# Narrower matmuls for the rest blocks of a two-layer MoE, an earlier request for a count, and scatters spread further apart

## The chip, the cores and the metric

The kernel runs on one core of one Trainium2 chip. The metric is the device time of one execution in microseconds (us); less is better. A core has TensorE (PE in the profile; its weight loads stand apart as PEld), VectorE (DVE), ScalarE (ACT), GpSimd (POOL) and SyncE (SP, which here only issues DMAs). Each runs its own queue of instructions in order, and they meet at semaphores.

## What is computed

A linear attention with decay, then two layers of a mixture of experts with one expert for each token. Cut to what matters:

```python
ret = (scale * q @ k.T) * Dmat               # 8 batches, 8 heads, 576 positions, 64 wide
x = (ret @ v)                                # as 4608 tokens of 512 columns
# layer 1, and layer 2 with other weights and a bias by modality:
logits = x @ w_gate
e_idx = argmax(logits)                       # one of 8 experts for each token
for e in range(8):
    h = maximum(x[e_idx == e] @ w1[e], 0)    # 512 -> 1024
    out[e_idx == e] = gate * (h @ w2[e])     # 1024 -> 512
```

With the reference's inputs the experts of the first layer get 602, 613, 589, 549, 586, 487, 608 and 574 tokens. The kernel takes tokens in blocks of 256 (pairs) and, for what is left over, in one block of up to 128 (the rest block). So each expert here has two pairs; all but expert 5 also have a rest, of 90, 101, 77, 37, 74, 96 and 62 tokens (the second pair of expert 5 covers the last 231). In the second layer two experts share all tokens (2315 and 2293).

## The kernel before, in words

**Attention and routing** (`attention_and_routing`). 36 chunks of 128 tokens, in four pairs of batches of nine chunks each. One chunk passes several engines: POOL scales v (`v_scale`, tile `vs`) and cuts the scores to a triangle (`a_cut`, two instructions on tile `a`); PE computes scores (`pa`), states (`pS`), output (`po`) and the transposed output with the gate's logits (`px`, `turned`); ACT and DVE move results between PSUM and SBUF (`og`, `xr`, `Sb`, `lg`). The order is written out by hand: every piece of work has a due time in chunks (`PLAN`), the list is sorted by it, and every engine gets its instructions in that order. Routing goes by groups of two to five chunks (they start at chunks 0, 4, 9, 13, 18, 22, 27, 31 and 34). When the last chunk of a group has its logits, `route` runs fifteen small steps (on DVE: `mx`, `dl`, `wq`, `m`, `oh`, `zz` and so on); then each chunk's rows are written to their expert's place in DRAM by an indirect DMA that POOL issues (`scatter`, tile `xs`, L178). The due times of a group's scatters are its last step plus 0.225 chunk, and 0.428 chunk from one to the next (`SCATTER`).

**The change over.** At the end of attention `counts` writes the experts' counts as small integers into `reg1`: pairs in columns 0 to 7, the rest flag in 8 to 15. All engines meet at a barrier, read their registers, and PE runs eleven matmuls (`READY`) on constants until the first rows arrive.

**The experts** (`experts`). Five engine programs, each walking through 16 positions (`P_`; 0 to 7 are the experts of the first layer, 8 to 15 those of the second), with branches on the counts. `walk` calls `unit(P_, s, w, ...)`: slot 0 and slot 1 are pairs of 256 columns, slot 2 is the rest block, always 128 columns in the first layer; in the second it may also be 64. For one unit:
- PE: the first product, `quarter(g)` for g = 0 to 3, each 24 matmuls (eight of 128 rows of w1, high and low halves in three combinations) into `ph[g]`; then, for each block of 128 tokens, the second product of 24 matmuls of 512 columns into `py`. For the second product the tokens are the stationary side, so its time doesn't depend on the columns of the first. Before each six matmuls of the first block it waits for a piece of hT (`h_full`).
- ACT: Relu of `ph[g]` to `hT` (high half, L1093); then `back`: Square of `py` and the scaled copy to `x2row`.
- DVE: the low half of `hT` (L1205); routing of the tokens for the second layer (`choose`, which ends in `oh`, and `place`); conversions of the next expert's weights (`conv`, `wb`); then `back` for each block, in the same queue.
- SP: loads and transposes, among them `x2T`, the transposed rows of finished blocks, which PE needs for the second layer's logits (L969).

The routing of a finished block is woven into the next units: in a rest block PE computes the logits of the pair's first block after the first six second-product matmuls and its ranks (L974, L975, which need `oh`) at the block's end; in a second pair the logits come after the third and fourth quarter, and the first ranks after the first six second-product matmuls.

In position 6 (`asked`) the order of the second layer's experts is settled ahead of time: after the first pair PE computes the counts so far (`counts(cums)`, L980), for which it waits for `cnt_ask` from DVE; DVE's `order()` turns them into an order. In the unit of the first pair DVE runs four pieces of hT, two conversions (`brought`), then the semaphore `cnt_ask`, then two `back`s, then `order()`.

Pieces of a program that are seldom taken (`co.unlikely`) are put at the end of the engine's program: a conditional jump leads there and another one back.

Of the kernel before, what the change touches and what calls it, by code (L numbers as in the profile page):

```python
# [14 lines left out]
I32 = mybir.dt.int32  # L15
AF = mybir.ActivationFunctionType
ALU = mybir.AluOpType
# [5 lines left out]
P = 128  # L23
# [15 lines left out]
GATES = -5.2, -1.440, -2.415, 1.091  # L39
WARM = 15  # L40
STEPS, RANKS, STEP, HURRY = 15, 10, 0.1684, {27: 0.1, 31: 0.055, NT - 2: 0.04}
SCATTER = 0.225, 0.428
HALVES = (38.2, 38.3, 38.32, 38.34, 38.36, 38.38, 38.4, 38.42), 43.0
READY = 11

# [37 lines left out]
def attention_and_routing(tc, st, I, K):  # L83

    nc = tc.nc
# [10 lines left out]
    ones, tri = K["ones"], K["tri"]  # L96
# [287 lines left out]
    for gr in groups:  # L384
        last = max(gr.start + n + PLAN["lg"] for n, x in enumerate(gr.items))
        chain = route(gr)
        for k in range(STEPS):
            last += HURRY.get(gr.start, STEP)
            if k == RANKS and gr.start < NT - 2:
                last = int(last - 0.045) + 1.045  # L390
            add(last, next, chain, None)
        for n, x in enumerate(gr.items):
            add(last + SCATTER[0] + n * SCATTER[1], scatter, x)
    def counts():

        pm = ps.tile([P, 512], F32, tag="pS", name="pm_cnt")
        nc.tensor.matmul(pm[:, 0:8], ones, cum[0], start=True, stop=True)
        cf = one.tile([1, 8], F32, tag="cf", name="cf")
        c2 = one.tile([1, 1, 8], I32, tag="c2", name="c2")
        reg = K["reg1"]  # L400
        nc.vector.tensor_copy(reg[:, 16:24], pm[0:1, 0:8])
        nc.vector.tensor_tensor(cf, pm[0:1, 0:8], col("eR")[0:1], op=ALU.subtract)
        nc.vector.tensor_scalar(c2[:, 0], cf, 127.0, None, op0=ALU.add)
        nc.vector.tensor_scalar(reg[:, 0:8], c2[:, 0], 8, None, op0=ALU.logical_shift_right)
        nc.vector.tensor_scalar(reg[:, 8:16], c2[:, 0], 6, 2, op0=ALU.logical_shift_right, op1=ALU.bitwise_and)


    fetch, high, low = first_weights(nc, I, K, lambda n: three.tile([P, 512], F32, tag="dqvk"[n % 4] + "n", bufs=6, name=f"w0s{n}"))
# [75 lines left out]
def experts(nc, st, I, K, out):  # L484
# [38 lines left out]
    take = T.take  # L523
    NP = 2 * E
    EP = 2
    PAIR, FULL, SMALL = 2 * P, P, P // 2

    def cols(P_, w):

# [2 lines left out]
    def count1(eng, R_, x):  # L532

        if x < E:
            eng.reg_load(R_["np"][x], reg1[0:1, x:x + 1])
            eng.reg_load(R_["od"][x], reg1[0:1, 8 + x:9 + x])

    def count2(eng, R_, x):

# [107 lines left out]
    def walk(co, R_, P_, unit, none=None, conv=None, first=None):  # L647

        eng, pairs, od = co.eng, R_["np"][P_ % E], R_["od"][P_ % E]
        if P_ < E:  # L650
            block, after = co.label("block"), co.label("after")

            def without():
                if none:
                    none()
                if first and P_ == 0:
                    first()
                for q in range(2 if conv and P_ == 0 else 0):
                    conv(0, 2 + q)
                if conv:  # L660
                    for slot in range(2):
                        for q in range(2):
                            brought(eng, R_, P_, conv, slot, q)

            def other():
                with when(eng, pairs, "GT", 1):
                    unit(P_, 1, PAIR, True, 1)
                    pairs_from(eng, R_, P_, unit, 2)
                if conv:
                    with eng.Else():  # L670
                        for q in range(2):
                            brought(eng, R_, P_, conv, 1, q)
            co.unlikely(pairs, "LT", 1, without, block)
            unit(P_, 0, PAIR, False, 0)
            co.unlikely(pairs, "NE", 2, other, block)
            unit(P_, 1, PAIR, True, 1)
            co.to(block)
            co.jump(od, "EQ", 0, after)
            unit(P_, 2, FULL, False)
            co.to(after)  # L680
            return
        with when(eng, pairs, "GT", 0):
            unit(P_, 0, PAIR, False, 0)
            with when(eng, pairs, "GT", 1):
                unit(P_, 1, PAIR, True, 1)
                pairs_from(eng, R_, P_, unit, 2)
        if none:
            with eng.Else():
                none()
        with when(eng, od, "EQ", 2):  # L690
            unit(P_, 2, FULL, False)
        with eng.Else():
            with when(eng, od, "EQ", 1):
                unit(P_, 2, SMALL, False)
        if conv:
            rest(eng, R_, P_, conv)
# [39 lines left out]
    def asked(P_, slot):  # L736

        return P_ == E - 2 and slot == 0

    def registers(rs, eng, tag, names, full=None):  # L740

        reg = lambda x: rs.enter_context(eng.register(f"{tag}{x}"))
        R_ = {x: reg(x) for x in names}
        for n in ("np", "od", "left"):
            R_[n] = [reg(f"{n}{x}") for x in range(E)]
        if full:
            eng.reg_load(R_["np"][0], reg1[0:1, 0:1])
            with when(eng, R_["np"][0], "GT", 1):
                full()
            eng.reg_load(R_["od"][0], reg1[0:1, 8:9])  # L750
        else:
            count1(eng, R_, 0)
        return R_

    with nc.Block() as block:
# [204 lines left out]
        def _(pe):  # L960
            with ExitStack() as rs:
# [69 lines left out]
                            counts(cums)  # L1031

                for n in range(READY):
                    pe.matmul(py[1], K["ones"], K["ones"].unsqueeze(1).to_broadcast([P, 4, P]), start=True, stop=True)
                pe.reg_mov(was, 0)
                co = Course(pe, "pe")
                for P_ in range(NP):
# [92 lines left out]
        def _(ve):  # L1130
            ch = Chain(ve, T, "dve")
            tt, ts, stt, tr = ve.tensor_tensor, ve.tensor_scalar, ve.scalar_tensor_tensor, ve.tensor_reduce
            with ExitStack() as rs:
# [64 lines left out]
                def unit(P_, s, w, sure, slot=None, routing=None):  # L1198
                    cs = cols(P_, w)
                    for g in range(4):  # L1200
                        routes = routing or behind(P_, slot)
                        if routes and g < 3:
                            routed(ve, was, s, sure, g, choose, 2)
                        take(ve, "hh_full")
                        stt(hT[:, 1, 2 * g:2 * g + 2, cs], ph[g][:, :, cs], 0.0, hT[:, 0, 2 * g:2 * g + 2, cs], op0=ALU.max, op1=ALU.subtract).then_inc(T["h_full"])  # L1205
                        if routes:
                            if g == 3:
                                routed(ve, was, s, sure, g, choose, 2)
                            routed(ve, was, s, sure, g, place, 2)
                        if P_ == 0 and slot == 0 and g < 2:  # L1210
                            conv(0, 2 + g)
                        if slot == 1 and g == 1:
                            brought(ve, R_, P_, conv, slot, 0)
                    for q in range(2 - (slot or 0)):
                        brought(ve, R_, P_, conv, slot, q + (slot or 0))
                    if routing or asked(P_, slot):
                        ve.sem_inc(T["cnt_ask"])
                    for b in range(blocks[s]):
                        back(s, b) if P_ < E else final(s, b)
# [146 lines left out]
def build(nc, I, off, outs):  # L1366
    with ExitStack() as st:
# [3 lines left out]
        K["ones"], K["tri"] = sb("ones", [P, P], F16), sb("tri", [P, P], F16)  # L1371
        K["wg2"] = sb("wg2", [P, 4, 24], BF16)
        K["bias"] = sb("bias", [P, 16], F32)
        K["reg1"] = sb("reg1", [1, 24], I32)
        K["zero"] = sb("zero", [P, XW], F32)
        K["wb0"] = sb("wb0", [P, 2, 8192], F16)
        K["xs1"] = nc.dram_tensor("xs1", [E * R, XW], F32, kind="Internal").ap()
# [50 lines left out]
```

## Time and profile before

| | us |
|---|---|
| median of 3 runs (1027.68 to 1029.19) | 1028.07 |
| the profiled execution | 1029.08 |
| its span in the trace | 1026.6 |
| PE busy, share of the span | 984.4, 96% |
| DVE busy | 465.6, 45% |
| ACT busy | 358.6, 35% |
| POOL busy | 234.8, 23% |

The mean granted clock of PE over the span was 0.98 of full speed. Attention fills the span up to some 194 us, the first layer from 211 to 633 us, the second one the rest. PE's row counts a matmul as busy until its modelled end, so a busy PE is not PE at its peak: the distance from one start to the next is the time that a matmul costs.

How the rows are read: a timeline row has the start, the duration, the engine, the line, the operation, what it writes and reads (out<-in), the shape and how many are merged (x8). In brackets stands how long the engine had been idle before, and what ended that; PEq or DVEq is the engine's own sequencer, that is, a wait or a branch ahead of the instruction. For a matmul the shape's second part is the moving side: 128x256 is 256 columns. In a table by windows, PEclk is the granted clock as a share of 2.4 GHz; 0.50 is 1.2 GHz.

### The profile page before, as it was taken

Reading aid. Unit: us, or ns where it says so; the run is one execution under the profiler, and the core shown is the slowest. Engines: PE = TensorE matmul, PEld = TensorE weight load, DVE = VectorE, ACT = ScalarE, POOL = GpSimd, SP = SyncE. Lnnn points to the kernel's source line nnn. Section 1 sums busy time; section 2 is a strip of 40 time slices with the busy share of each in tenths; the row PEclk is TensorE's granted clock in tenths of the full one; section 3 lists DMA queues with packets and bytes.
Section 4 is the critical chain, followed back from the end, with each engine's and each line's share of the span. In section 5 each row is a group of like instructions: output and inputs, shape, how many; then the busy total and the mean of one; then the engine's idle time right before and its main releaser. Section 6 shows DMA issues by size and latency. Waiting matters only on the chain. (4 is left out here: it accounts for less than half of the span.)

```text
span 1026.6 us, 23918 instructions
## 1 busy us (share of the span) xinstructions
PE 984.4 (96%) x8529; PEld 708.7 (69%) x8529; DVE 465.6 (45%) x1420; ACT 358.6 (35%) x701; POOL 234.8 (23%) x308
## 2 busy tenths in 40 slices
PE   8998999399999999999999999999999999999996
PEld 6998898357667676767666767666776666776673
DVE  4666766666565656565656565323111111111111
ACT  3564554344444444343534343223111121111111
POOL 6566655510121111111112111101100101100110
PEclk9999999789999999999999999999999999999998
DMA  8887875279739383747665564361222211112100
GB/s 326 302 295 245 276 246 177 96 238 269 187 60 244 76 234 84 190 114 172 216 169 142 111 185 97 113 173 53 52 42 51 72 34 52 53 41 62 52 31 24
DMA packets 180256, 145.10 MB, mean 141 GB/s; under 512 B 136569, under 2 KB 136733, under 8 KB 180128
## 3 DMA queue, kind: packets, MB, share of 16 engines
q1 hardware_dynamic: 171168, 114.89, 42.2%
q0 software_dynamic: 8960, 28.62, 7.4%
q8 instruction: 67, 1.10, 0.4%
q14 instruction: 61, 0.50, 0.2%
HBM read 80.46 MB, written 33.92 MB: 111 GB/s over the span
## 5 line engine op out<-in xcount | busy, mean ns | idle before, releaser
L991 PE MATMUL ph<-xT,wb 128*128 128x256 f16 (+2 forms) x1344 | 338.0, 262 | 0.1
L993 PE MATMUL ph<-xT,wb 128*128 128x256 f16 (+2 forms) x1344 | 338.0, 262 | 0.0
L992 PE MATMUL ph<-xT,wb 128*128 128x256 f16 (+2 forms) x1344 | 338.0, 262 | 0.0
L1205 DVE SCALAR_TENSOR_TENSOR hT<-ph,hT 128x512 f16<-128x512 f32 (+2 forms) x168 | 105.8, 637 | 332.2 <-DVEq L457 332.1
L1001 PE MATMUL py<-wb,hT 128*128 128x512 f16 x608 | 230.4, 379 | 0.0
L1000 PE MATMUL py<-wb,hT 128*128 128x512 f16 x608 | 230.3, 379 | 0.0
L999 PE MATMUL py<-wb,hT 128*128 128x512 f16 x608 | 230.3, 379 | 0.0
L1093 ACT ACTIVATE hT<-ph 128x512 f16<-128x512 f32 (+2 forms) x168 | 92.4, 551 | 200.9 <-ACTq L457 200.7
L991 PEld LDWEIGHTS ph<-xT,wb 128*128 128x128 f16 x1344 | 131.3, 98 | 16.3 <-issue 0.4
L992 PEld LDWEIGHTS ph<-xT,wb 128*128 128x128 f16 x1344 | 131.3, 98 | 16.0
L993 PEld LDWEIGHTS ph<-xT,wb 128*128 128x128 f16 x1344 | 131.4, 98 | 12.7
L1331 POOL DMA_INDIRECT out_dram<-yo,idxo x37 | 35.9, 969 | 334.3 <-POOLq L457 334.3
L1001 PEld LDWEIGHTS py<-wb,hT 128*128 128x128 f16 x608 | 59.4, 98 | 71.8
L999 PEld LDWEIGHTS py<-wb,hT 128*128 128x128 f16 x608 | 59.3, 98 | 63.4
L1000 PEld LDWEIGHTS py<-wb,hT 128*128 128x128 f16 x608 | 59.4, 98 | 63.2
L1320 POOL TENSOR_SCALAR idx<-v_pos 128x1 int32<-128x1 f32 x39 | 22.2, 570 | 325.8 <-POOLq L457 325.8
L469 DVE SCALAR_TENSOR_TENSOR wb<-stg,wb 128x2048 f16<-128x2048 f32 x38 | 86.9, 2287 | 10.2 <-DVEq L457 9.7
L1087 ACT ACTIVATE yo<-py,v_gcol 128x512 f32<-128x512 f32 x37 | 25.4, 688 | 168.2 <-ACTq L457 168.2
L1070 ACT ACTIVATE wb<-stg 128x2048 f16<-128x2048 f32 x38 | 72.3, 1902 | 0.9 <-ACTq L457 0.9
L1324 POOL DMA_INDIRECT xs<-x2row,idx x39 | 44.4, 1137 | 37.5 <-POOLq L457 37.5
L331 PE MATMUL px<-iw,og 128*128 128x144 f32 x288 | 46.0, 304 | 6.7 <-DVE og L326 6.7
L1084 ACT ACTIVATE x2row<-py,v_s 128x512 f16<-128x512 f32 x39 | 26.8, 687 | 71.6 <-ACTq L457 71.6
(152 smaller groups left out, 977.0 us busy)
## 6 DMA issues: line engine op xcount, KB each, us to landing
stg<-in_moe_w_dram SPq DMA_DIRECT2D x38, 1024.0 KB, 5.0
qn<-in_q_dram SPq DMA_DIRECT2D x36, 256.0 KB, 5.0
dkn<-in_dk_dram SPq DMA_DIRECT2D x36, 256.0 KB, 5.1
vn<-in_v_dram SPq DMA_DIRECT2D x36, 256.0 KB, 5.1
kn<-in_k_dram SPq DMA_DIRECT2D x32, 256.0 KB, 5.1
xs<-zero SPq DMA_DIRECT2D x8, 262.0 KB, 2.2
xs<-zero SPq DMA_DIRECT2D x8, 258.0 KB, 2.4
w0s<-in_moe_w_dram SPq DMA_DIRECT2D x8, 256.0 KB, 5.8
```

Source lines behind the costliest of these rows:

```text
L331: nc.tensor.matmul(px[:, hp, 0:IW], self.og[:, hp, :], iw[:, hp, :], start=True, stop=True)
L469: r = fn(*a, **kw).then_inc(self.sem, 1)
L991: pe.matmul(o, w1(P_, 0)[:, c, fs], xT[s][:, c, cs], start=(c == 0), stop=False)
L992: pe.matmul(o, w1(P_, 0)[:, c, fs], xT[s][:, 4 + c, cs], start=False, stop=False)
L993: m = pe.matmul(o, w1(P_, 1)[:, c, fs], xT[s][:, c, cs], start=False, stop=(c == 3))
L999: pe.matmul(py[b], hT[:, 0, f, bs], w2(P_, 0)[:, f, :], start=(f == 0), stop=False)
L1000: pe.matmul(py[b], hT[:, 0, f, bs], w2(P_, 1)[:, f, :], start=False, stop=False)
L1001: m = pe.matmul(py[b], hT[:, 1, f, bs], w2(P_, 0)[:, f, :], start=False, stop=(f == 7))
L1070: ac.activation(wb[P_ % 2][:, 0, 2048 * c:2048 * c + 2048], stg[:, 2048 * c:2048 * c + 2048], AF.Copy, scale=WS).then_inc(T["cv_full"])
L1093: ac.activation(hT[:, 0, 2 * g:2 * g + 2, cs], ph[g][:, :, cs], AF.Relu).then_inc(T["hh_full"])
L1205: stt(hT[:, 1, 2 * g:2 * g + 2, cs], ph[g][:, :, cs], 0.0, hT[:, 0, 2 * g:2 * g + 2, cs], op0=ALU.max, op1=ALU.subtract).then_inc(T["h_full"])
L1324: po.indirect_dma_start(out=xs2, out_offset=bass.IndirectOffsetOnAxis(ap=idx[b], axis=0), in_=x, in_offset=None, bounds_check=E * R - 1, o ...
```

## The change

- PE's program gets a register `wd` for each expert: (count + 127) >> 5, its two lowest bits, from a new operation in `counts` and a new column of `reg1`. In the first layer the rest block's first product runs over 32, 64, 96 or 128 columns. 96 stands in line; the other three are put at the end of PE's program, each behind a compare and jump (`co.unlikely`). ACT and DVE go on with 128 columns. As columns of `ph` that no matmul has written are then read, PE's eleven warming matmuls write to all four `ph` instead of `py[1]`.
- DVE signals `cnt_ask` in position 6 ahead of the two conversions instead of behind them.
- The scatters of the groups that start before chunk 22 get due times 0.9 chunk apart instead of 0.428.

```diff
-SCATTER = 0.225, 0.428
+SCATTER, APART, LATE = 0.225, (0.9, 0.428), 22
...
-            add(last + SCATTER[0] + n * SCATTER[1], scatter, x)
+            add(last + SCATTER + n * APART[gr.start >= LATE], scatter, x)
...
+        nc.vector.tensor_scalar(reg[:, 24:32], c2[:, 0], 5, 3, op0=ALU.logical_shift_right, op1=ALU.bitwise_and)
...
-    PAIR, FULL, SMALL = 2 * P, P, P // 2
+    PAIR, FULL, SMALL, PART = 2 * P, P, P // 2, P // 4
...
+            if "wd" in R_:
+                eng.reg_load(R_["wd"][x], reg1[0:1, 24 + x:25 + x])
...
-            unit(P_, 2, FULL, False)
+            if "wd" in R_:
+                for v in (3, 1, 0):
+                    co.unlikely(R_["wd"][P_], "EQ", v, lambda w=PART * (v + 1): unit(P_, 2, w, False), after)
+                unit(P_, 2, 3 * PART, False)
+            else:
+                unit(P_, 2, FULL, False)
...
-        for n in ("np", "od", "left"):
+        for n in ("np", "od", "left", "wd") if tag == "pe" else ("np", "od", "left"):
...
-                    pe.matmul(py[1], K["ones"], K["ones"].unsqueeze(1).to_broadcast([P, 4, P]), start=True, stop=True)
+                    pe.matmul(ph[n % 4].rearrange("p f t -> p (f t)"), K["ones"], K["ones"].unsqueeze(1).to_broadcast([P, 4, P]), start=True, stop=True)
...
+                    if asked(P_, slot):
+                        ve.sem_inc(T["cnt_ask"])
                     for q in range(2 - (slot or 0)):
                         brought(ve, R_, P_, conv, slot, q + (slot or 0))
-                    if routing or asked(P_, slot):
+                    if routing:
                         ve.sem_inc(T["cnt_ask"])
...
-        K["reg1"] = sb("reg1", [1, 24], I32)
+        K["reg1"] = sb("reg1", [1, 32], I32)
```

## Rows read from the trace of the kernel before

**Rows 1.** Head of the page.

```profile
span 1026.6 us, 23918 instructions
```

**Rows 2.** Waits of PE from 211 to 1010 us: total, times, longest.

```profile
PE pr L980 <- PEq L457: 1.8, 1, 1.8
```

**Rows 3.** Timeline of PE at a 128-column rest block and a 64-column one.

```profile
307.19 0.38 PE L1001 MATMUL py<-wb,hT 128*128 128x512 f16 x1
307.40 0.22 PE L991 MATMUL ph<-xT,wb 128*128 128x128 f16 x1
...
312.76 0.38 PE L999 MATMUL py<-wb,hT 128*128 128x512 f16 x1
...
821.19 0.19 PE L991 MATMUL ph<-xT,wb 128*128 128x64 f16 x1
...
823.99 0.38 PE L999 MATMUL py<-wb,hT 128*128 128x512 f16 x1
```

**Rows 4.** Timeline of DVE beside the rest block of expert 1.

```profile
310.11 0.74 DVE L469 SCALAR_TENSOR_TENSOR x2row<-py,v_s,x2row 128x512 f16<-128x512 f32 x1
311.54 1.13 DVE L1205 SCALAR_TENSOR_TENSOR hT<-ph,hT 128x256 f16<-128x256 f32 x3 [0.68 <-DVEq L457]
...
315.81 0.29 DVE L469 TENSOR_SCALAR oh<-w_w,v_m,cur 128x8 f16<-128x8 f32 x1
```

**Rows 5.** Timeline of PE in the rest block of expert 0.

```profile
258.75 0.38 PE L999 MATMUL py<-wb,hT 128*128 128x512 f16 x1
...
260.57 0.35 PE L969 MATMUL pr<-wg,x2T 128*128 128x24 bf16 x8 [0.37 <-PEq L457]
```

**Rows 6.** Windows of PE: stretch, length, busy, PEclk, DMA share, GB/s.

```profile
84.00:86.00 2.00, 1.55 (x12) 0.66 0.02 7
86.00:88.00 2.00, 2.00 (x16) 0.50 0.16 22
182.00:184.00 2.00, 1.21 (x18) 1.00 0.59 233
```

**Rows 7.** Timeline of PE: px of the same chunks in three pairs of batches.

```profile
34.67 1.25 PE L331 MATMUL px<-iw,og 128*128 128x144 f32 x8
...
44.27 1.00 PE L331 MATMUL px<-iw,og 128*128 128x144 f32 x6
...
75.75 1.25 PE L331 MATMUL px<-iw,og 128*128 128x144 f32 x8
...
82.85 1.25 PE L331 MATMUL px<-iw,og 128*128 128x144 f32 x8 [2.38 <-DVE og L326]
...
89.91 1.25 PE L331 MATMUL px<-iw,og 128*128 128x144 f32 x8
...
121.39 1.25 PE L331 MATMUL px<-iw,og 128*128 128x144 f32 x8
...
134.78 1.25 PE L331 MATMUL px<-iw,og 128*128 128x144 f32 x8
```

**Rows 8.** Timelines of DVE and POOL beside the first hole.

```profile
77.70 3.79 DVE L201 TENSOR_TENSOR oh<-wq,m 128x32 f16<-128x32 f32 x1
...
80.40 1.04 POOL L269 TENSOR_TENSOR vs<-vn,cst 128x512 f32<-128x512 f32 x1
```

**Rows 9.** Timelines of PE and DVE in expert 6.

```profile
545.18 0.17 PE L980 MATMUL pr<-cums,ones 128*128 128x8 f16 x1 [1.81 <-PEq L457]
...
558.78 0.29 DVE L469 TENSOR_SCALAR oh<-w_w,v_m,cur 128x8 f16<-128x8 f32 x1
...
559.27 0.17 PE L974 MATMUL pr<-oh,tri 128*128 128x8 f16 x1
```

**Rows 10.** Page, parts 3 and 6: a DMA queue's packets and MB; issues, us to landing.

```profile
q8 instruction: 67, 1.10, 0.4%
...
meta<-xs SPq DMA_DIRECT2D x16, 12.0 KB, 2.1
```

**Rows 11.** Timeline of PE behind the skipped rest block of expert 5.

```profile
521.88 0.27 PE L991 MATMUL ph<-xT,wb 128*128 128x256 f16 x1
```

## The prediction, as put on record before the result

> **What bounds the kernel now.** I read the page first: the span is 1026.6 us [rows 1]. The profiled execution took 1029.08 us, so 2.5 us lie around the span; the median of the three runs, 1028.07 us, lies 1.0 us under that execution, and I subtract the sum from the median, taking its pieces from the span. Then the waits of TensorE (PE) between 211 and 1010 us, the two expert layers: beside one wait of 1.8 us [rows 2] there is next to nothing. So there PE sets the time, and only what shortens PE's own work, or its one wait, counts. What one cannot see in that view is who stands close behind PE; for that I read the rows of ScalarE (ACT) and VectorE (DVE) against those of PE. In the attention stage (0 to 194 us) PE is also nearly full, but its timeline has holes, near 80 and 126 us, where the engines behind it are late [rows 7, 8]. The whole change acts on these three places.
>
> **Rest blocks (part one).** A rest block has 96 first-product matmuls and 24 second-product ones. With 128 columns the first product took 312.76 - 307.40 = 5.36 us (56 ns a matmul), with 64 columns, in the second layer, 823.99 - 821.19 = 2.80 us (29 ns) [rows 3]. So the price is linear, 1.28 us for each 32 columns. The rests are 90, 101, 77, 37, 74, none, 96 and 62 tokens, so the widths are 96, 128, 96, 64, 96, none, 96, 64, and PE's own work falls by 4 x 1.28 + 2 x 2.56 = 10.2 us.
>
> But the second product needs hT. In expert 1 the block began at 307.40, which is also when the pair block before it ended. That pair's second half still has to pass ACT and DVE (the last of it on DVE ends at 310.11 + 0.74 = 310.85) before DVE comes to the rest block's first hT, 311.54; three of them took 1.13 us, so it is done some 0.4 us later, 4.54 us after the block's start [rows 4]. None of this depends on the rest block's own matmuls, and the diff leaves it alone. From DVE's end to PE's next matmul I take 0.20 us (oh done at 558.78 + 0.29 = 559.07, matmul at 559.27, rows 9). So the second product can't start before 4.74 us, whatever the width: 0.6 us under 5.36. Experts 2, 3 and 4 get 0.6 each. Expert 0 gets nothing: after its first six second-product matmuls (0.215 us each, 307.40 - 307.19 in rows 3: 258.75 + 1.29 = 260.04) PE waited for transposed rows until 260.57 [rows 5]; arriving earlier only lengthens that. Experts 6 and 7 I put at half, 0.25 each (0 to 0.6). Together -2.3 us (-0.5 to -3.6); the other 8 us become a wait of PE.
>
> Two things are then added. First, that wait: about 0.7 us with 96 columns, 4.74 - 2.80 = 1.9 us with 64. PE's granted clock fell to half after the hole of 2.4 us before 82.85 [rows 7] (0.66 and 0.50 in the two slices behind it) and not in the slice with a hole of 0.8 us at 182 [rows 6]; the fall cost 0.34 x 2 + 0.50 x 2 = 1.7 us. So the 64-column blocks stand at the edge, and I take one fall in the two: +1.7 (0 to 3.4). Second, the 64- and 128-column versions stand at the end of PE's program, so three blocks jump out and back. No row shows such a far jump; the nearest is the skipped rest block of expert 5, with no idle time before the next matmul at 521.88 [rows 11]. That jump, like the one out, lies under some 5 us of matmuls already handed over. The jump back doesn't: PE's sequencer passes its last wait when oh is there, 315.81 + 0.29 = 316.10 [rows 4], and the block ends at 312.76 + 24 x 0.215 + 0.2 (the small matmuls between) = 318.1, 2.0 us later. A transfer of about a code page's size (16 KB: 1.10 MB in 67) took 2.1 us to land [rows 10]. 2.1 against 2.0, with waits and the first matmul behind it: 0.3 each, +0.9 (0 to 2.1 each). The three compares a block and one register load an expert are PE sequencer work under 24 matmuls of 0.215 us; nothing, unless the cover is gone, as at the start (below). Part one in all: -2.3 + 1.7 + 0.9 = +0.3 us.
>
> On the jump the Trainium skill (Runtime: NRT & Kernel Launch, Instruction fetch mechanics) speaks against this change: a taken branch whose target is not among the pages at hand must fetch it before going on. The row of the skipped block shows no stall, but it is a short jump forward; no row of this kernel shows the long ones. This is the rival "jumps" below.
>
> **The count asked for earlier (part two).** In expert 6 PE waited 1.81 us until 545.18 for the count [rows 9], which DVE asks for only behind two conversions. Asked for ahead of them, the count is free, since nothing else holds it. So PE gains those 2 us, and what the clock lost behind them. Where does it go? DVE's chain from the conversions through the two returns, the ordering, hT and the choice that ends in oh (559.07) runs without a wait for PE, and the ask moves no work of it. PE's rank matmul at 559.27 came 0.20 us after oh [rows 9]: DVE was already just as late. So PE, however early, waits there until the same 559.27. Gain 0. The hole now lies behind the first product, 3 to 4 us long, and the half clock falls on work that PE must do: 1.2 us of the 1.7, since some of it may pass while PE still waits. Part two: +1.2 us (0 to +1.7).
>
> **Scatters spread (part three).** In the second pair of batches two chunks run from 75.75 to 89.91, 14.16 us; the same chunks of the first pair, which has no scatters there, took 44.27 - 34.67 = 9.60; those of the third pair 134.78 - 121.39 = 13.39 [rows 7]. Lost: 4.56 + 3.79 = 8.35 us. The reason: DVE's oh, 32 elements, lasted 3.79 us, from 77.70 to 81.49: to the end of a string on GpSimd (POOL) without a pause: a scatter, vs, two cuts, and the vs that ends at 80.40 + 1.04 = 81.44 [rows 8]. og stands behind it, px behind og; then the clock falls. The fourth pair's loss stays, as its groups keep their spacing.
>
> Sorted by its due times, POOL's order becomes cut, vs, scatter, cut, vs, scatter instead of two scatters, vs, cuts, vs. Each row keeps its duration, so in the second pair the strings become: cuts to about 77.98, a pause, a scatter from 78.15, vs to 80.2. DVE's oh ends in the pause; the next such operation, zz, comes at about 78.2, beside the scatter. If it gets through, all 8.35 us come back. If it is held to the end of vs, 2.0 us, og comes some 1.0 us late; a hole of 1.0 us brings no half clock by rows 6. I take half, 0.5 in each pair: -7.3.
> The Trainium skill (SBUF — State Buffer, Terms) says that the port pair which DVE and GpSimd share is held for one full instruction. By it DVE would lose at most one POOL instruction, some 1.05 us, and all 8.35 us come back; the row, with DVE held over several instructions of a string, says otherwise.
>
> The spread puts something new elsewhere: in three other places (groups 0, 9 and 18) the last scatter now lies between a cut and vs, right where the following group's dl is due. If dl is held until vs ends, 1.0 us, about 0.8 reaches PE; I take 0.4 each, +1.2 (0 to 2.4). Part three: -7.3 + 1.2 = -6.1 us (-8.4 to -3.9).
>
> **The change over to the experts.** One more small DVE operation before the eight weight remainders, on which the last scatter and the barrier wait, and one more register load ahead of PE's eleven warming matmuls: no row has the load; between 0.1 and 0.6, taken as +0.4. The other target of the warming matmuls changes no time, as nothing waits on either.
>
> **Sum.** -6.1 + 0.4 + 0.3 + 1.2 = -4.2: 1028.07 - 4.2 = 1023.9 us, its own range 1020.5 to 1027.
>
> **The rivals.**
> "All of the scatters": zz gets through, dl too, and no half clock at the 64-column blocks: -8.35 + 0.4 - 2.3 + 0.9 + 0 = -9.4, 1018.7 us. For it: the pauses of POOL; against: the string at 77.70.
> "The scatters move the stall": each string still holds DVE for 2.0 us or more, with a half clock behind both holes and dl held three times: -8.35 + 2 x (1.0 + 1.7) + 3 x 0.8 = -0.55 instead of -6.1: 1029.4 us. For it: DVE was held across four instructions; against: POOL then has pauses that it has not now.
> "The rest blocks give all they have": if the first hT came earlier than 4.54 us, part one would be -10.2 + 0.9: -13.8 in all, 1014.3 us. Against it: rows 4, which the diff doesn't touch.
> "Jumps", the slower end: every jump out or back costs PE a page's 2.1 us, six times 12.6 instead of 0.9: +7.5, 1035.6 us. The place is the first matmul of the two 64-column blocks and the 128-column one, and the one after each; it decides from about 1.2 us a jump ((4.2 + 2.1 + 0.9) / 6). For it: the code lies far from its caller; against: rows 11 and the matmuls handed over ahead.
>
> **How the numbers follow.** Forecast 0.58, all of the scatters 0.12, rest blocks in full 0.06, stall moved 0.17, jumps 0.07. A measurement of this kernel can tell 0.2% (2.06 us) from no change. Faster by more: 0.54 + 0.12 + 0.06 = 0.72; within: 0.04 of the forecast and 0.14 of the moved stall, 0.18; slower: 0.03 + 0.07 = 0.10. The range of 8 in 10 takes in the forecast, "all of the scatters" and the moved stall, and leaves out the other two: 1018.5 to 1029.5.
>
> **What would show it.** In the profile after: in the experts' layers PE now waits at the rest blocks' second product, and its first row stands 4.7 to 4.8 us after the block's start in 64- and 96-column blocks alike (wrong if it follows at 4.1 and 2.8). The count's matmul follows without a wait, and a hole of 3 to 4 us stands before the rank matmul of expert 6's second pair (wrong if PE runs through). The holes at 80 and 126 us shrink to at most 1 us, oh and zz under 2.1 us, and the chunks take 9.6 to 11 us instead of 14.2 and 13.4. The first matmul behind expert 1's, 3's and 7's blocks comes within 0.5 us; one of 2 us would make the forecast wrong, as would DVE still held for over 3 us.

## The result and the profile after

| | before | after |
|---|---|---|
| median, us | 1028.63 (1027.68 to 1029.93, 4 runs) | 1040.83 (1038.44 to 1045.48, 4 runs) |
| profiled execution | 1029.08 | 1045.48 |
| its span | 1026.6 | 1043.0 |

The change makes the kernel slower: ratio 1.0111 (95%: 1.0091 to 1.013), some 11 us. I had expected 1023.9 us and at most 1029.5. The profiled execution of after is the slowest of its four, so its pieces are set against its own time: 1043.0 - 1026.6 = 16.4 us are to be found in it.

First the waits of PE in the two layers (what was waited for, total us, times, longest), where before had one wait of 1.8 us and little else [rows 2]:

```profile
PE ph L999 <- PEq L458: 6.1, 1, 6.1
PE ph L1001 <- issue: 4.9, 1, 4.9
PE pr L977 <- PEq L458: 4.8, 4, 3.0
PE py L1007 <- PEq L458: 4.2, 6, 1.2
PE pr L982 <- PEq L458: 2.5, 1, 2.5
PE ph L1000 <- issue: 1.4, 2, 0.8
```

The line numbers have moved by 8: L999 to L1001 is the first product, L1007 the second, L977 the logits, L982 the ranks. Two waits in the *first product* lead the list, which is neither hT nor the ask. "issue" says that PE waited for nothing that the profile shows. The timeline of PE has them at the ends of two rest blocks that jump, expert 1's (above the dots) and expert 3's:

```profile
319.44 0.17 PE L983 MATMUL pr<-cum,ones 128*128 128x8 f16 x1
325.68 0.37 PE L999 MATMUL ph<-xT,wb 128*128 128x256 f16 x1 [6.07 <-PEq L458]
...
435.21 0.27 PE L1000 MATMUL ph<-xT,wb 128*128 128x256 f16 x1
440.35 0.27 PE L1001 MATMUL ph<-xT,wb 128*128 128x256 f16 x1 [4.87 <-issue]
```

Expert 1's block is done at 319.44; nothing comes for 6.2 us. Expert 3's jump back takes 0.3 us (433.50 to 433.80), so its target was at hand: two matmuls run, then PE stands for 5.1 us, and the following page of code arrives within that time (437.89 to 438.90). What lies in the first hole, by windows (length, busy, PEclk, DMA share, GB/s):

```profile
317.00:319.00 2.00, 2.00 (x11) 1.00 0.96 371
319.00:321.00 2.00, 0.61 (x5) 1.00 1.01 404
321.00:323.00 2.00, 0.00 (x0) 1.00 1.32 125
323.00:325.00 2.00, 0.00 (x0) 0.91 1.28 78
325.00:327.00 2.00, 1.32 (x7) 0.50 1.58 309
327.00:329.00 2.00, 2.00 (x11) 0.50 0.92 187
329.00:331.00 2.00, 2.00 (x18) 0.50 0.99 366
```

The DMA engines are full with the next expert's weights when the jump comes, and behind the hole PE runs at half clock. The trace also keeps the records of PE's sequencer, which the views leave out: the branch begins at 317.88 and lasts until 325.22. The transfers by queue, from there to 321.3 us and then to 323.9 us, show when the code is fetched (packets, MB, share):

```profile
q1 hardware_dynamic: 516, 1.33, 100.0%
...
q1 hardware_dynamic: 602, 0.18, 161.2%
q8 instruction: 1, 0.02, 6.0%
```

The instruction queue moves nothing for 3.4 us, then one page, which takes 2.5 us; PE's next instruction comes at 325.28, 7.4 us after the start of the branch. Over the whole run the page has nine fetches more than before [rows 10]:

```profile
q8 instruction: 76, 1.25, 0.5%
```

Set piece by piece against before (from the start of one unit to the next on PE), the 16.4 us are these:

| piece | expected | profiled run |
|---|---|---|
| narrow blocks of experts 2, 4, 6 (no jump) | -1.45 | -1.95 |
| expert 0's rest block | 0 | +3.25 |
| expert 1 (jump, 128 columns) | +0.3 | +8.67 |
| experts 3 and 7 (jump, 64 columns) | +1.45 | +7.49 |
| the ask: hole gone, new hole | +1.2 | -2.21 + 1.84 |
| attention and change over | -5.7 | -2.20 |
| two other pairs that wait for transposed rows | 0 | +1.42 |
| sum | -4.2 | +16.3 |

In the attention row 1.67 us are a later first chunk (18.64 instead of 16.97 us), which came and went between runs of kernels that are alike there: 16.96 in one and 18.86 in another on the same chip.

### The profile page after: what moved, and what is told of

It is laid out like the page before. It is cut to its first block, busy times and chain, and to the rows that moved or that the text cites. A ratio compares the mean times of both kernels' runs of the same rounds, so it can differ in the third digit from the quotient of the medians.

```text
span 1043.0 us, 23947 instructions
## 1 busy us (share of the span) xinstructions
PE 978.8 (94%) x8529; PEld 698.7 (67%) x8529; DVE 465.4 (45%) x1421; ACT 357.1 (34%) x701; POOL 234.6 (22%) x308
## 5 line engine op out<-in xcount | busy, mean ns | idle before, releaser
L999 PE MATMUL ph<-xT,wb 128*128 128x256 f16 (+3 forms) x1344 | 329.4, 261 | 6.1 <-PEq L458 6.1
L1001 PE MATMUL ph<-xT,wb 128*128 128x256 f16 (+3 forms) x1344 | 329.5, 261 | 4.9 <-issue 4.9
L1000 PE MATMUL ph<-xT,wb 128*128 128x256 f16 (+3 forms) x1344 | 329.5, 261 | 1.4 <-issue 1.4
L1007 PE MATMUL py<-wb,hT 128*128 128x512 f16 x608 | 231.5, 381 | 4.2 <-PEq L458 4.2
L999 PEld LDWEIGHTS ph<-xT,wb 128*128 128x128 f16 x1344 | 131.1, 98 | 28.3 <-issue 12.1
L1001 PEld LDWEIGHTS ph<-xT,wb 128*128 128x128 f16 x1344 | 131.2, 98 | 13.2
L1007 PEld LDWEIGHTS py<-wb,hT 128*128 128x128 f16 x608 | 59.5, 98 | 68.7 <-issue 5.7
```

The costliest lines, as they stand in the source:

```text
L999: pe.matmul(o, w1(P_, 0)[:, c, fs], xT[s][:, c, cs], start=(c == 0), stop=False)
L1000: pe.matmul(o, w1(P_, 0)[:, c, fs], xT[s][:, 4 + c, cs], start=False, stop=False)
L1001: m = pe.matmul(o, w1(P_, 1)[:, c, fs], xT[s][:, c, cs], start=False, stop=(c == 3))
L1007: pe.matmul(py[b], hT[:, 0, f, bs], w2(P_, 0)[:, f, :], start=(f == 0), stop=False)
```

## The experiments

The theory now (A): the jumps, by the fetch of code. Rivals: (B) the narrow blocks, their holes and half clocks; (C) the scatters and the ask. With the first result the runs came in five sets, on several chips. The kernel before took 1028.6 to 1039.3 us in them, and on one chip 1030.2 in one set and 1039.1 in the next, so totals are compared only as ratios to before in the same set; between traces only the lengths of single pieces are compared. In the diffs "..." stands for lines that are left out; those of the jumps alone and the light transfers are against after, the others against before. Where nothing else is said, the ask and the scatters are as in before.

**Widths alone.** Part one of the diff without the moved ask and the spread scatters.

> The widths alone (part one with its count), the ask and the scatters as before. Theory A, jumps: three blocks jump out of PE's program and back, and the code that is jumped to has to be fetched. In the trace of after this cost experts 1, 3 and 7 together some 16 us, and the half clock behind is in it; the attention stage's gain is missing here, so about 1043 us (1039 to 1047), and after the blocks of experts 1 and 3 holes of 4 to 7 us. Rival B, narrow blocks: what is lost is lost at the second product of the narrow blocks (held by hT), by the half clock behind such holes, and by expert 0's late transposed rows; also about 1043 us, this run does not tell A from B. Rival C, the scatters and the ask make the loss: 1027 to 1030 us here.

1.0141 (1.0107 to 1.0175), +14.5 us, with holes of 7.3 and 4.6 us at the same two places. The loss is all in part one; C is out.

**Jumps alone.**

```diff
-                    co.unlikely(R_["wd"][P_], "EQ", v, lambda w=PART * (v + 1): unit(P_, 2, w, False), after)
-                unit(P_, 2, 3 * PART, False)
+                    co.unlikely(R_["wd"][P_], "EQ", v, lambda w=FULL: unit(P_, 2, w, False), after)
+                unit(P_, 2, FULL, False)
```

> The jumps alone: the same four versions in the same places, chosen by the same count, but each 128 columns wide, so no block is narrower than before. Theory A: the loss stays, 1036 to 1045 us, with the holes at the jumps back of experts 1 and 3 (4 to 7 us each) and at the jumps out (0.4 to 1 us each), while experts 0, 2, 4 and 6, which do not jump, take what they took before. Rival B: nothing narrow, nothing lost: 1028 to 1030 us. Rival C: 1028 to 1030 us.

1.0166 (1.013 to 1.0201), with nothing narrow in it, and the holes stand where they stood:

```profile
318.89 0.17 PE L983 MATMUL pr<-cum,ones 128*128 128x8 f16 x1
323.62 0.37 PE L999 MATMUL ph<-xT,wb 128*128 128x256 f16 x1 [4.56 <-PEq L458]
...
433.86 0.27 PE L1000 MATMUL ph<-xT,wb 128*128 128x256 f16 x1
438.31 0.37 PE L1001 MATMUL ph<-xT,wb 128*128 128x256 f16 x1 [4.18 <-issue]
```

**Narrow without jumps.**

```diff
-            unit(P_, 2, FULL, False)
+            unit(P_, 2, 3 * PART if co.tag == "pe" else FULL, False)
```

> Narrow without jumps: PE multiplies every rest block of the first layer in 96 columns, in line, with no other version; leaves out expert 1's last 5 rows, whose hT is not written. Theory A: experts 1 to 7 gain 0.6 to 0.7 us each (-3.9), expert 0 between 0 and +3.3 (if its transposed rows come late again): 1024.5 to 1028.5 us, no hole over 2 us at a block's end. Rival B: the narrow blocks cost more than they give; six holes, and the half clock behind some: 1031 to 1038 us. Rival C: 1024.5 to 1028.5 us, like A.

0.9981 (0.9962 to 0.9999), 2 us faster. No hole over 1.1 us at a block's end, and no half clock in the first layer beyond the one of before. PE's waits for hT and for the transposed rows (total, times, longest) stay short:

```profile
PE py L999 <- PEq L457: 3.9, 7, 0.8
PE pr L969 <- PEq L457: 2.9, 4, 0.9
```

The rest blocks are 4.8 us shorter in this trace, and four pairs behind them 2.9 us longer, as they now wait for transposed rows. These three runs settle it: A holds, B falls.

**Scatters alone.**

> The scatters' spacing alone. Theories A and B: the attention stage of after: two chunk pairs 3.2 and 2.5 us shorter, one pair that loses its half clock 1.0 shorter, three new losses of 0.9 each: -3.9 us, 1024.7 us (1023.5 to 1026.5). Rival C: the scatters make part of after's loss, 1030 us or more, by something that they delay behind the attention stage.

0.9961 (0.9946 to 0.9975): 4.0 us faster (2.6 to 5.6), as expected.

**What in a jump costs: distance?** The versions in line instead of at the program's end, each skipped by a short branch:

```diff
-            unit(P_, 2, FULL, False)
...
+                for v in (2, 3, 1, 0):
+                    on = co.label("version")
+                    co.jump(R_["wd"][P_], "NE", v, on)
+                    unit(P_, 2, PART * (v + 1), False)
+                    co.eng.br(after)
+                    co.at(on)
...
```

> The four widths without a far jump: the versions stand in line one behind the other (96, 128, 64, 32 columns), each skipped by a short branch, and a block that is done branches over those that follow. A version is about one code page (the fetches of 16 KB). Theory A1, it is the jump as such: whatever is not among the pages already fetched has to be fetched, however near, and the branch at a block's end skips two or three pages: holes of 4 to 7 us behind the blocks of experts 0, 1, 2, 4 and 6, the half clock behind them, 1046 to 1065 us. Theory A2, it is the distance: short branches are free, as the skipped block of expert 5 was before: 1025 to 1030 us. Rival B (the narrow blocks) has fallen with the runs before and expects 1028 to 1032.

1.0422 (1.0399 to 1.0445), the slowest of all: holes of 2.3 to 9.2 us behind the blocks of experts 0 to 4 and 6, and more at the branches out of experts 3 and 7. The worst, expert 1's, and one behind a skip of a single version (expert 3's end):

```profile
333.40 0.17 PE L986 MATMUL pr<-cum,ones 128*128 128x8 f16 x1
342.64 0.37 PE L1002 MATMUL ph<-xT,wb 128*128 128x256 f16 x1 [9.07 <-issue]
...
461.77 0.27 PE L1002 MATMUL ph<-xT,wb 128*128 128x256 f16 x1
464.34 0.27 PE L1003 MATMUL ph<-xT,wb 128*128 128x256 f16 x1 [2.30 <-issue]
```

So it does not take a far jump: behind a skip of about a page of code (a rest block lasts 10.8 us, and in before fetches of 16 KB mostly come every 10 to 16 us in the first layer) PE can already stand. At expert 3's end the branch itself took 0.4 us, and the page that PE stood for landed at 462.99.

**The weight transfers ahead of the fetch.** The jumps alone, with small weight transfers (from expert 2 on the experts compute with leftover weights):

```diff
...
+                    if P_ > 1:
+                        w, src = w[:, 0:1, 0:P], src[:, 0:1, 0:P]
```

> The jumps alone, all versions 128 columns wide, but with small weight transfers: from expert 2 on only 1/8 to 1/16 of each weight piece is loaded, so the experts compute with leftover weights; all waits stay. In the run with the jumps alone PE's instruction fetch at the jump back of expert 1 began 3.4 us behind the branch, beside weight transfers that kept all DMA engines busy, and 0.9 us behind the branch at the jump out, with the DMA engines idle. Theory A-queue: the fetch stands behind the weight transfers; it now begins about 1 us behind the branch, and the hole of expert 1 falls from 4.7 to 1.5 to 2.5 us (3.8 us of jump less 2.0 us of matmuls handed over), that of expert 3 from 4.5 likewise. Theory A-fixed: a jump back takes its 6 to 7 us whatever the DMA engines do; both holes stay over 4 us.

Expert 1's hole falls from 4.7 to 2.8 us, expert 3's only from 4.5 to 3.9. Their rows:

```profile
330.69 0.17 PE L986 MATMUL pr<-cum,ones 128*128 128x8 f16 x1
333.52 0.37 PE L1002 MATMUL ph<-xT,wb 128*128 128x256 f16 x1 [2.66 <-PEq L458]
...
446.09 0.37 PE L1004 MATMUL ph<-xT,wb 128*128 128x256 f16 x1 [3.63 <-issue]
```

The fetch now begins 1.7 us behind the branch (329.04, 330.75). That is not the 1 us that I expected, and the windows say why: other transfers, such as the transposes of rows, still fill the engines behind the branch.

```profile
329.00:330.00 1.00, 1.00 (x6) 1.00 1.21 276
330.00:331.00 1.00, 0.86 (x6) 1.00 0.87 198
331.00:332.00 1.00, 0.00 (x0) 1.00 0.00 0
```

From branch to next instruction, in the traces of four kernels:

| jump | DMA share, windows from the branch on | branch to fetch | fetch | to the next instruction | total |
|---|---|---|---|---|---|
| jumps alone, expert 1, out | 0.05, 0.00 | 0.9 | 0.9 | 1.6 | 3.4 |
| light transfers, expert 1, out | 0.07, 0.00 | 0.9 | 1.1 | 1.6 | 3.6 |
| after, expert 1, out | 0.14, 0.00 | 0.9 | 1.4 | 1.5 | 3.8 |
| light transfers, expert 1, back | 1.21, 0.87 | 1.7 | 0.9 | 1.4 | 4.1 |
| jumps alone, expert 1, back | 1.00, 1.03, 1.20 | 3.4 | 1.0 | 1.5 | 6.0 |
| after, expert 1, back | 0.96, 1.01 | 3.5 | 2.5 | 1.4 | 7.4 |
| widths alone, expert 1, back | 1.03, 1.01, 0.99 | 3.7 | 3.3 | 1.5 | 8.6 |

The last part is nearly the same everywhere; the first grows with what the DMA engines do, the second in two of the jumps back. So the fetch stands behind data transfers, for expert 1. At expert 3 it also began earlier with the light transfers, 2.3 us after the branch instead of 3.8, but PE went on only 2.3 us after it had landed instead of 1.4. Why, and so why this hole shrank by only 0.6 us, stays open. That run's total (1.0121) says nothing, as leftover weights change the second layer's counts.

**Which branches show: two versions in line.** 128 columns first, for expert 1, then 96 for the others.

```diff
...
+                co.jump(R_["wd"][P_], "NE", 3, narrow)
+                unit(P_, 2, FULL, False)
+                co.jump(R_["wd"][P_], "EQ", 3, after)
+                co.to(narrow)
+                unit(P_, 2, 3 * PART, False)
```

> Two versions in line: the one of 128 columns first, for expert 1, which then branches over the other (about one code page); the rest branch over the first version, take 96 columns and run straight on. Theory A1, a branch costs when its target is not yet fetched and what it costs shows when PE has fewer matmuls handed over than the fetch takes: the six branches out lie under 4 to 5 us of matmuls and cost at most 0.9 us each, probably nothing; expert 1's branch at the block's end lies under 2 us and leaves a hole of 2 to 7 us with the half clock behind it. With 0.65 us saved by each of six narrow blocks: between 2 us less and 9 us more than before, ratio 0.998 to 1.009, likeliest 1.002. Rival, one version is near enough: no hole, ratio 0.996 to 0.9985.

1.0124 (1.0098 to 1.0151), more than I expected. Expert 1's branch at its end left 4.9 us. The branches out of experts 2, 3, 4, 6 and 7 left nothing (2.1 to 2.2 us from branch to next instruction for experts 2 to 4, 0.4 to 0.5 for 6 and 7, under the matmuls handed over). Two more showed: expert 0's branch out, beside weight transfers (DMA share 0.96 and 1.06, 6.1 us from branch to instruction), and the skip of expert 5, which now has two versions to pass and lost 2.0 us where one version lost nothing [rows 11]. Expert 0's branch:

```profile
262.65 0.38 PE L1012 MATMUL py<-wb,hT 128*128 128x512 f16 x1
265.36 0.20 PE L1002 MATMUL ph<-xT,wb 128*128 128x96 f16 x1 [2.32 <-PEq L458]
```

**Branches inside fetched code: small skips.** One version, whose quarters multiply the last 32 columns only if the count asks for it:

```diff
...
+                        if w == 3 * PART:
+                            on = co.label("narrow")
+                            co.jump(R_["wd"][P_], "NE", 3, on)
+                            columns(g, slice(w, P))
+                            co.to(on)
+                        columns(g, cs).then_inc(T["ph_full"])
```

> One version whose four quarters each multiply the last 32 columns only if the count asks for them: every narrow block branches four times over some 3 KB of code, inside a page or to the next, which is fetched ahead. Theory A1: the branches cost no fetch; six blocks save 0.65 us each, expert 1 pays for 96 more matmuls of 32 columns, between nothing (5.36 us as before) and 1.5 us (as if each took what a matmul of 64 columns takes): ratio 0.9955 to 0.9995, and up to 3 us more if expert 0's transposed rows are late again. Rival, a taken branch costs 2 us or more as such, wherever it goes: 24 of them, ratio over 1.02.

1.0066 (1.0043 to 1.0088): slower than theory A1 had it and far under the rival's 1.02. The 24 short branches are not the cause. Experts 2, 3 and 4, with four taken branches each, took 10.13 us from block to next unit, 0.66 less than before, as in after. As these blocks wait for hT, the first product alone tells more: in expert 2 its 96 matmuls took 4.04 us, and 4.03 in line without a branch. So a taken branch as such costs nothing that shows. Expert 1 paid 1.1 us, as a matmul of 32 columns costs 25 ns, not a quarter of the 56 of 128 columns. The rest: a hole of 1.6 us in expert 0's first product, where a page of code was late (it came from 261.88 to 264.49, the next matmul at 265.91); 1.8 us at expert 5, whose rest block has become longer and is skipped whole; and waits for transposed rows, 1.8 us in expert 0 and 2.5 us, with a half clock, behind expert 2. With the better scatters (below) added:

> The small skips and the scatters of the full-step run (1.0 for the groups at 4 and 13, 0.9 for 22) in one kernel. Theory: the gains add, 0.9916 for the scatters and 0 to 4 us for the skips: ratio 0.988 to 0.9916. Rival: the narrow blocks' gain is lost again at the transposed rows, of which several experts were already late by 0.8 to 1.2 us in the full-step run: 0.9905 to 0.994, no better than the scatters alone.

0.9967 (0.9953 to 0.9981): on the rival's side, and worse than its range. In the trace six narrow blocks give 2.9 us; pairs that wait for transposed rows take 3.3, the skip of expert 5 takes 2.0, expert 1's extra matmuls 1.1 and the first unit 0.6. That is 4.0 us more than before in the two layers.

**The ask alone.**

> The earlier ask alone. Theory: the count comes without a wait, and the hole moves from the count's matmul to the rank matmul of expert 6's second pair, since DVE's chain to that pair's choice is not shortened: 0 to 0.5 us less (ratio 0.9995 to 1.0), +1.2 us (1.0012) if the half clock falls behind the new hole. Rival: the wait of 1.8 us is simply gone: ratio 0.998, and no hole over 1 us in that pair.

1.0017 (1.0002 to 1.0031), no gain, as forecast. PE's rank matmul now comes behind a wait of 2.4 us, at 558.48:

```profile
PE pr L974 <- PEq L457: 2.4, 1, 2.4
```

It is 0.8 us earlier than in before, and 0.5 us of that were there already at the first expert matmul (210.70, 211.20). The unit ahead of the wait is 2.21 us shorter, the one with it 2.20 us longer.

**Where the scatters' new losses come from.** Spacing 0.9 only for the groups at 4 and 13, then also for 22:

```diff
-            add(last + SCATTER[0] + n * SCATTER[1], scatter, x)
+            add(last + SCATTER + n * APART[gr.start not in (4, 13)], scatter, x)
```

> The scatters' spacing of 0.9 only for the two groups of five chunks whose scatters met the next group's routing (those that start at chunks 4 and 13); the groups at 0, 9 and 18 keep 0.428. Theory: the three new losses of 0.9 us each go, the rest of the gain stays: 2.7 us faster than with the spacing in all five, so 6.5 us under before (ratio 0.9935, 0.992 to 0.995). Rival: the new losses come from the scatters of the groups at 4 and 13 themselves, or the gain needs all five: no better than 0.996.

> As the run with two groups, and the same spacing for the group that starts at chunk 22, whose scatters meet the fourth pair's chunks (6.84 and 6.47 us where the other pairs now take 5.48 each). Theory: the fourth pair shortens like the second and third, by 2.4 us: 9 us under before (ratio 0.991, 0.9895 to 0.993). Rival: the last groups' routing comes earlier, and the spread scatters then push POOL's or DVE's work past the end of the attention stage: what the pair gains is lost at the change over, ratio 0.993 to 0.996.

0.9951 (0.9936 to 0.9966) and 0.9943 (0.9929 to 0.9956), in a set in which every kernel that was traced lost 0.8 us at three other chunks and 5 to 6 us at the end of attention. In the traces the step is as expected: the chunks behind the groups at 0, 9 and 18 take 4.65 + 5.0 us again instead of 5.02 + 5.52, and group 22 shortens its first chunk from 7.07 to 5.39. By the ratios, the first step is worth less than I wrote and the second too. In the trace of the second the last chunk took 1.0 us more than in that of the first (8.59, 7.55), which would fit its rival. Once more on another chip, where that chunk took 4.98 us, and beside it a spacing of 1.0:

```diff
+            add(last + SCATTER[0] + n * {4: 1.0, 13: 1.0, 22: 0.9}.get(gr.start, SCATTER[1]), scatter, x)
```

> The spacing of 0.9 for the groups at 4, 13 and 22 once more, beside the next kernel on the same chip. Expected: 1.5 us more on PE's path in each of the three pairs than in the first pair without scatters (about 5.5 + 5.5 us for two chunks against 9.6), since DVE's zz is held for 1.6 us behind a scatter and vs; ratio 0.991 to 0.9945.

> The groups at 4 and 13 with a spacing of 1.0 instead of 0.9 (22 with 0.9): every scatter then keeps its place behind vs, where 0.9 moves the fourth and fifth ahead of vs. Theory, DVE is held by what follows a cut or a scatter without a pause: zz meets only vs, is held for 0.5 us instead of 1.6, and two pairs gain up to 1.2 us each: 2 us under the run with 0.9 (1 to 2.6). Rival, the string counts, not its order: the scatters behind vs make strings as long, and the two kernels are equal within 0.7 us.

0.9927 (0.9908 to 0.9946) and **0.9916 (0.9897 to 0.9935)**: 1021.9 us beside 1030.2 of before, the best of all kernels here. The step from 0.9 to 1.0 is 0.5 us in each of two pairs, less than I wrote, and their intervals overlap. The timelines of DVE and POOL with 0.9:

```profile
77.03 0.96 DVE L196 SCALAR_TENSOR_TENSOR wq<-dl,cst 128x32 f32<-128x32 f32 x1
...
78.61 1.63 DVE L203 TENSOR_TENSOR zz<-lg,oh 128x32 f32<-128x32 f32 x1
...
78.11 0.99 POOL L178 DMA_INDIRECT xs<-xr,pi  x1 [0.17 <-issue]
79.12 1.06 POOL L269 TENSOR_TENSOR vs<-vn,cst 128x512 f32<-128x512 f32 x1
```

and with 1.0:

```profile
76.97 1.97 DVE L196 SCALAR_TENSOR_TENSOR wq<-dl,cst 128x32 f32<-128x32 f32 x1
...
79.56 0.18 DVE L203 TENSOR_TENSOR zz<-lg,oh 128x32 f32<-128x32 f32 x1
...
76.66 1.22 POOL L317 TENSOR_SCALAR_AFFINE_SELECT a<-a 128x512 f32<-128x512 f32 x2
77.84 1.04 POOL L269 TENSOR_TENSOR vs<-vn,cst 128x512 f32<-128x512 f32 x1
79.05 1.01 POOL L178 DMA_INDIRECT xs<-xr,pi  x1 [0.17 <-issue]
```

With 0.9 zz ends with vs; with 1.0 it runs in 0.18 us beside a scatter that nothing follows, but wq then lasts through the cuts to the end of vs: 1.97 us. The string counts, and here only a part of it was moved out of the way.

> The earlier ask, and a spacing of 1.0 for the groups at 4, 13 and 22. Theory: the sum of its parts, as the run with the full step, 0.4 us less for the ask and between 1 us less and 1 us more for the last group, whose scatters now end later: ratio 0.988 to 0.992. Rival: the fourth pair's scatters push the last groups' routing and with it the change over to the experts: no better than the run with 0.9, 0.9925 to 0.9945.

0.9924 (0.9904 to 0.9944): no better than the run with 1.0 and 0.9. The ask gives nothing here either: in the trace 2.21 us go and 2.21 come back one unit later. Nor does the wider spacing of the last group: from the first px to the last it took 162.53 us, and 162.48 without.

## Why the prediction was wrong

**The step that failed** is the price of a jump back: "A transfer of about a code page's size (16 KB: 1.10 MB in 67) took 2.1 us to land [rows 10]. 2.1 against 2.0 ... 0.3 each, +0.9 (0 to 2.1 each)." The cover of 2.0 us was nearly right: between expert 1's branch and its last matmul lie 1.6 us. The price was not. The row was the nearest one, but not of the same thing in two ways. Landing of a small load is only a middle part of a jump: with the DMA engines nearly idle it took 3.4 to 3.8 us from branch to next instruction. And it was a median over the run, while expert 1's jump back came when the DMA engines were full with the next expert's weights; there it took 6.0 to 8.6 us. At expert 3 it was the page behind the jump's target that was late, which the sum has no term for. On top came what the sum had put down for the 64-column blocks only: the half clock behind a long hole (2.25 us in the pair behind expert 1's block, by the windows above and the pair's 24.06 us against 21.81). In all, the two jumps back cost 8.5 and 6.7 us in the profiled run, where the sum had 0.3 each. I had set the upper bound of the term by the same row, so the range could not hold the result.

Rows 11 misled me as well. That skip passes one version, and no hole followed; I let it speak for jumps in general. With two versions to pass the same skip lost 2.0 us.

**The rival "jumps"** had the mechanism and the side, with 2.1 us for each of six; I gave it 0.07. Measured, the six are uneven: 0.2 and 8.5 for expert 1 (hole and clock), none and 6.7 for expert 3. Expert 7's block took 1.2 us more than before: a hole of 0.96 us inside its version and one of 1.35 ahead of the second product, with a half clock behind; its jump back left next to nothing (0.3 us in the next pair). The rule that I set beside it (the Trainium skill, Runtime: NRT & Kernel Launch, Instruction fetch mechanics: a taken branch to a page not at hand must fetch it first) agrees with these runs: the branch at 317.88 ended 1.4 us after its page had landed. It gives no time for it; the runs do.

**Rest blocks.** That hT holds them was right: the second product came 4.69 us after the start with 96 columns (371.08 to 375.77) and 4.71 with 64 (424.96 to 429.67), where I had 4.74. The gain was 0.66, 0.66 and 0.62 us for experts 2, 4 and 6, for 0.6, 0.6 and 0.25. One of the two 64-column blocks brought a half clock, as taken, but the number was luck: the holes ahead of it were 0.96 and 1.35 us, not the 1.9 that I had counted on, and one of them is the code's. Expert 3's block had holes of 0.86 and 1.09 us and no half clock. The rival "all they have" is out. Expert 0 was wrong: PE waited 3.0 us for its transposed rows, with a half clock behind (0.50 and 0.70 in the two slices from 260 us); they were issued 3.07 us into the block and took 5.8 us, where before it was 2.07 and 4.8. The width alone does not explain it, since the run with 96 columns in line had no wait there; the widths alone had 1.8 us, the jumps alone, with the same compares, none. It was not tried apart, and stays open.

**The ask.** Gain 0 was right: the hole moved in front of the rank matmul. The half clock that I added to it did not come in after (a wait of 2.45 us, not a hole of 3 to 4), nor in the trace of the ask alone; its ratio, 1.0017, would have room for it in other executions, which is not shown.

**Scatters.** The two pairs took 10.96 and 10.94 us instead of 14.16 and 13.39 [rows 7], so 5.7 us came back where I took 7.3. The price of the new places was twice what I wrote: 0.9 each, not 0.4. That makes -3.0 by these pieces and -4.0 (-5.6 to -2.6) by the run alone, instead of -6.1. After's fourth pair was another 1.0 us shorter (5.46 instead of 6.47 us in one chunk), but so it was in the widths alone, where no scatter was moved. At 83.79 us px still came 0.76 us late: zz was held for 1.64 us, as I had weighed it ("held to the end of vs"), but in full and not by half, and wq took 0.96.

**The change over** cost 0.1 us (PE's last attention product 2.29 us earlier, the first expert's 2.20), for 0.4.

## What to carry over

A branch on PE is priced by three things in its own place: whether its target and the page behind that are already fetched (here a skip of 24 matmuls always found it so, a skip of one version only at times), how many microseconds of work are handed over when the sequencer takes it, and what the DMA engines do at that moment. Put a choice between versions where the cover is long, or make the skip small; here even that did not pay, as expert 1's full block and the skip of expert 5 became longer and waits for transposed rows took the rest. Do not take a price for it from a row with another load on the DMA engines. A saving on an engine that waits for another right behind it is worth only the distance to that wait, here 0.66 of 1.3 to 2.6 us; measure that first.

## What the runs showed of the hardware

- A taken branch to code not yet fetched, from the branch to the next instruction: 3.4 to 3.8 us on PE with nearly idle DMA engines, 6.0 to 8.6 us beside weight transfers. Four taken branches over the code of 24 matmuls each: no cost that shows (4.04 us against 4.03 for the first product).
- First-product matmuls start every 56 ns (128 columns), 42 (96), 29 (64) and 25 (32): in proportion down to 64, hardly less below.
- DVE's wq lasted 1.97 us beside the cuts and vs and ended with them. The Trainium skill (SBUF — State Buffer, Terms) has the port pair that DVE and GpSimd share held for one full instruction; if DVE came in between two, some 1.05 us, a vs, would be the most (an estimate). Here the measurement decides: DVE is held through a string, and zz ran beside a scatter that stands alone in 0.18 us.
- The same kernel differs between sets of runs: before took 1028.6 to 1039.3 us, and on one chip 1030.2 and then 1039.1. In the two sets that took longest every kernel that was traced lost time at the same chunks of the attention stage (5.0 us instead of 4.2 at three of them, 6.4 and 7.6 to 8.6 instead of 4.0 and 5.0 at the last two). Why stays open.
